# Wide zero-weight fillers in the open PV group, conv lags by modelled time, later VectorE PV

## Chip, cores, metric

One core of one Trainium2 chip. The metric is the device time of one execution in microseconds (us); lower is better. TensorE is called PE here, VectorE DVE, ScalarE ACT, as in the profile.

## The reference, cut to what matters

```python
# A: attention, S=2048, D=512, 32 heads of 16
scores = einsum("bhqd,bhkd->bhqk", q, k) * Dh**-0.5
o = softmax(scores) @ v ; a = o @ wo
# B: H3 block: short shift conv, then a causal conv of length 2048 per channel (by FFT)
kv = k_shift * v
y  = irfft(rfft(kv) * rfft(ssm_k))[:S] + kv * ssm_D
b  = q * y
return concatenate([a, b], -1)
```

2048 blocks of 128x512 scores need an exponential each. The long conv is done on PE, as 8192 small matmuls in the gaps of the attention ("lags": 4 matmuls each, one per column tile).

## The kernel before

The whole program is laid out in advance in steps T. In each step PE does scores (QK) of one chunk of 2 or 3 blocks, PV (the exponentials times `v`) of an older chunk, then background work: lags of the conv, and in some steps, called slots, a query or output projection. The sums of PV stay open in their bank over many steps, one group of sums per column tile (a strip of 32 columns) of PE's array; ACT does the exponentials (tile PT in the profile), and DVE takes one block of some chunks by a polynomial (tile PTD). Fillers are matmuls with zero weights, which compute nothing and only keep PE busy. The host code keeps a modelled time for each engine (`pe.t`, `at(handle)`) and places work by it. The score banks are two sets of three, so scores of T+1 wait for the exponentials of T-1.

```python
LAGS, PACE, END = 7, 1.08, 24
N_SLOT, MARGIN, WINDOW, BUSY = 35, 0.25, 3.4, 0.56

# pv_step: PV of DVE blocks only when modelled as ready for 0.3 us
d = [b for b in d if b in h_blk and (close or at(h_blk[b]) <= pe.t - 0.3)]

# emit_bg: conv lags of one step
st["lags"] = min(st["lags"] + PACE * st["left"] / max(NT - END - T, 1), 3.0 * LAGS)
left = min(LAGS, int(st["lags"]), int((room(T) - 0.06) / 0.055))

def warm_up(T):                       # fillers, to keep PE busy
    if T <= max(early) or T >= NT - 14:
        return
    gap = at(h_exp[T - 1]) + 0.25 - max(pe.t, at(bank_free[BGB]) + 0.12)
    lately = sum(r for t, r in pe.runs[-40:] if t > pe.t - WINDOW)
    n = min(int(gap / 0.055), 4, int((BUSY * WINDOW - lately) / 0.054))
    ...                               # n matmuls, 128 columns, into the conv bank

for T in range(NT + 3):               # (cut)
    emit_qk(T); pv_step(T); emit_bg(T); warm_up(T)
```

The softmax here doesn't subtract the row's maximum and nothing guards it: scores larger than these inputs give would overflow.

## Time and profile before

| | before |
|---|---|
| time, three runs | 924.28 to 926.37 us, median 926.11 |
| granted PE clock, mean | 0.951 |
| first to last exponential | 902.6 us, of which 77.0 us above the undisturbed period |
| stretches at half clock | 18, about 90 us |
| fillers | 234 of 128 columns, 12.5 us of streaming |

ACT bounds the kernel (94% busy, 56% of the chain that ended last); the question is why its exponentials come later than they could. The clock rows of the traces of this kernel hold only 0.5 and 1.0, and every stretch between the first and the last (34 of them) lasts a whole multiple of 3.413 us. "Half-clock time" is therefore 2 x (1 - mean granted clock) x time. "Streaming" is columns over 2.4 per ns: 512-column matmuls of the projections (L761) follow each other by 0.216 us at full clock (median in the trace of the kernel before), which is 2.37 per ns. "Standstill" is a gap of over 1.2 us on PE's matmul row after 105 us and before the tail.

### The profile page before, as it was taken

The page shows a single profiled execution, that of the slowest core. Times are in us where ns is not written, and L with a number is a line of the kernel's source. Part 1 is how long each engine was busy: PE and PEld are TensorE (multiplying, and loading weights), DVE is VectorE, ACT ScalarE, POOL GpSimd, SP SyncE. Part 2 cuts the span into 40 slices and gives each one's busy share as a digit, 9 for nine tenths or more (in the row PEclk, how much of TensorE's full clock was granted, in tenths as well). Part 3 has the DMA queues.
Part 4 walks back from the last instruction along what each step waited for, and adds up shares of the span by engine and source line. Part 5 has one row for each costly group of instructions (what it writes and reads, how often), then busy time and mean ns, then how long its engine had stood idle before and what let it go on. Part 6 is the DMA issues. An engine that isn't in the chain of part 4 may idle for free.

```text
span 921.7 us, 29467 instructions
## 1 busy us (share of the span) xinstructions
PE 752.7 (82%) x13091; PEld 331.8 (36%) x13137; DVE 781.2 (85%) x1293; ACT 867.7 (94%) x724; POOL 42.3 (5%) x62
## 2 busy tenths in 40 slices
PE   8988788888888888788887887888877888777787
PEld 3322224333334343434443333333433433333332
DVE  4788798899979698999897797889899898899972
ACT  5998999999999999999999898999999999999997
POOL 2113030000000000000000000000000000000000
PEclk9997998898999898999999799899999999999999
DMA  9743459999999999999999999899999999989610
GB/s 312 242 137 114 160 211 339 368 399 378 375 372 408 342 391 348 408 364 405 350 380 406 327 391 345 308 404 400 356 368 361 343 307 389 363 297 367 228 46 23
DMA packets 88512, 295.65 MB, mean 321 GB/s; under 512 B 11205, under 2 KB 19394, under 8 KB 88002
## 3 DMA queue, kind: packets, MB, share of 16 engines
q1 hardware_dynamic: 82114, 280.13, 81.6%
q0 software_dynamic: 3872, 12.58, 4.0%
q8 instruction: 104, 1.70, 0.7%
q10 hardware_dynamic: 2400, 1.05, 0.4%
q14 instruction: 22, 0.18, 0.1%
HBM read 287.31 MB, written 6.42 MB: 319 GB/s over the span
## 4 chain that ended last, share of the span: by engine, by line
ACT 56%; PE 24%; DVE 11%; DMA 5%; issue 3%; SPq 1%; ACTq 0%; DVEq 0%
ACT PT L562 56%; PE PS L550 8%; PE PS L639 5%; DMA WR<-kz_scratch 5%; DVE EH L599 4%; PE PS L811 3%; PE PS L761 2%; PE PS L376 2%; DVE FX L592 1%; PE PS L362 1%; PE PS L369 1%; DVE PTD L604 1%; DVE DT L708 1%; SPq L207 1%; DVE QT L391 1%
## 5 line engine op out<-in xcount | busy, mean ns | idle before, releaser
L562 ACT ACTIVATE PT<-PS 128x1536 bf16<-128x1536 f32 (+1 forms) x718 | 863.7, 1381 | 40.9 <-PE PS L550 39.7
L550 PE MATMUL PS<-QT,KTo 32*128 32x512 bf16 x2048 | 291.5, 400 | 123.6 <-ACT PT L562 108.7
L811 PE MATMUL PS<-WR,KV 128*16 128x128 bf16 (+15 forms) x8192 | 243.8, 230 | 17.9 <-DMA WR<-kz_scratch 7.0
L599 DVE SCALAR_TENSOR_TENSOR EH<-EH,FX 128x512 f32<-128x512 f32 x374 | 257.5, 705 | 0.8
L639 PE MATMUL PS<-PT,VAF 128*32 128x512 bf16 x1861 | 230.6, 409 | 10.1 <-DVE DT L708 4.8
L811 PEld LDWEIGHTS PS<-WR,KV 128*11 128x11 bf16 (+15 forms) x8192 | 173.6, 110 | 90.2 <-issue 64.7
L592 DVE TENSOR_SCALAR FX<-PS 128x512 f32<-128x512 f32 x187 | 131.6, 704 | 57.0 <-PE PS L550 56.7
L550 PEld LDWEIGHTS PS<-QT,KTo 32*128 32x128 bf16 x2048 | 71.0, 91 | 284.9 <-ACT PT L562 226.5
L604 DVE SCALAR_TENSOR_TENSOR PTD<-EH,FX 128x512 uint16<-128x512 f32 x187 | 132.0, 711 | 6.2 <-PE PS L639 5.2
L599 DVE SCALAR_TENSOR_TENSOR EH<-FX 128x512 f32<-128x512 uint16 x187 | 129.5, 702 | 0.8
L639 PEld LDWEIGHTS PS<-PT,VAF 128*32 128x32 bf16 x1861 | 54.3, 94 | 138.3 <-issue 116.0
L639 PE MATMUL PS<-PTD,VAF 128*32 128x512 bf16 x187 | 59.0, 406 | 0.0
L708 DVE STREAM_TRANSPOSE DT<-PS 128x512 f32<-128x512 f32 x31 | 22.7, 733 | 17.9 <-PE PS L639 17.5
L761 PE MATMUL PS<-WKV,OTN 128*128 128x512 bf16 x114 | 31.7, 388 | 2.7 <-issue 1.9
L828 DVE CAST YB<-PS 128x512 bf16<-128x512 f32 x32 | 22.1, 689 | 13.5 <-PE PS L811 13.3
L362 PE MATMUL PS<-xT,WQP 128*128 128x512 bf16 x107 | 28.4, 380 | 5.2 <-issue 1.9
L207 POOL DMA_DIRECT2D out_dram<-OUTA x12 | 6.6, 554 | 565.2 <-DVE OUTA L770 565.2
L970 PE MATMUL PS<-IDN,ZW 128*9 128x128 bf16 (+12 forms) x234 | 31.0, 234 | 0.6 <-PE PS L639 0.4
L391 DVE TENSOR_SCALAR QT<-PS 128x512 bf16<-128x512 f32 x32 | 22.6, 705 | 7.2 <-PE PS L362 6.6
L725 DVE STREAM_TRANSPOSE OTN<-DTN 128x512 bf16<-128x512 bf16 (+1 forms) x35 | 23.3, 674 | 0.1
L406 DVE CAST VAF<-PS 128x512 bf16<-128x512 f32 x16 | 11.1, 691 | 12.1 <-PE PS L376 12.1
L369 PE MATMUL PS<-xT,WKV 128*128 128x512 bf16 x60 | 18.1, 427 | 1.8 <-DVE QT L391 1.1
(66 smaller groups left out, 269.1 us busy)
## 6 DMA issues: line engine op xcount, KB each, us to landing
WR<-kz_scratch SPq DMA_DIRECT2D x512, 512.0 KB, 8.1
WR<-in_B_k_dram POOLq DMA_DIRECT2D x16, 256.0 KB, 4.6
kz_scratch<-WR SPq DMA_DIRECT2D x1, 2176.0 KB, 9.1
KV<-in_A_x_dram SPq DMA_DIRECT2D x4, 512.0 KB, 7.3
QN<-in_B_q_dram POOLq DMA_DIRECT2D x2, 1024.0 KB, 12.8
out_dram<-QN POOLq DMA_DIRECT2D x2, 1024.0 KB, 8.7
WR<-in_B_v_dram SPq DMA_DIRECT2D x6, 256.0 KB, 2.8
QT<-in_B_k_dram POOLq DMA_DIRECT2D x6, 256.0 KB, 4.8
```

Of the source, the lines that this page charges most:

```text
L362: return e.matmul(PS[:, bank, :], lhsT=WQP[:, dc, g, :], rhs=xT[:, dc, qb * 512:(qb + 1) * 512], start=(dc == 0), stop=(dc == 3))
L391: hh = urgent(lambda e: e.tensor_scalar(QT[:, qb % 2, g, :], PS[:, bank, :], QSCALE, None, ALU.mult), [h, h_kzt[0] if qb == 1 else None], ...
L550: ins = e.matmul(PS[:, bank, :], lhsT=KTo[32 * s:32 * s + 32, g // 2, kt * 128:(kt + 1) * 128], rhs=QT[32 * s:32 * s + 32, qb % 2, g, :], ...
L562: h_exp[T] = act.op(lambda e: e.activation(PT[:, T % R_PT, 0:n * QB], PS[:, banks[0]:banks[0] + n, :].rearrange("p b f -> p (b f)"), ACT.E ...
L592: h_f = urgent(lambda e: e.tensor_scalar(fx, PS[:, bank, :], FIX_ADD, FIX_HI, ALU.add, ALU.min), [h, h_last.get(i - R_FX)], slack=0.6)
L599: st["h"] = dve.op(lambda e: e.scalar_tensor_tensor(eh, src, (A3, A2, A1)[j], frac, ALU.add, ALU.mult), [st["h"], h_last.get(i - R_EH), h_ ...
L604: lambda e: e.scalar_tensor_tensor(out16, eh, A4, fx, ALU.mult, ALU.add),
L639: ins = e.matmul(dst, lhsT=w, rhs=rhs, start=(k == 0), stop=(k == KT - 1), tile_position=(0, 32 * s))
L708: h_t = urgent(lambda e: e.transpose(out=dt, in_=PS[:, pvb(n), :]), [h] + before, slack=0.1, us=(0.63, 0.751))
L761: ins = e.matmul(PS[:, bank, :], lhsT=OTN[:, oslot(qb * NG + g), t * 128:(t + 1) * 128], rhs=WOP[:, g, :], start=(g == 0), stop=(g == NG - 1))
L811: ins = e.matmul(PS[32 * c:32 * c + NB - n, BGB, 128 * (kk % 4):128 * (kk % 4) + 128], lhsT=KV[:, n:NB, d], rhs=WR[:, d % R_W, 128 * (NB - ...
L970: ins = e.matmul(PS[0:rows, BGB, 128 * kk:128 * kk + 128], lhsT=ZW[:, 0:rows], rhs=IDN[:, :], start=(lag == 0), stop=(lag == 0), tile_posi ...
```

## The change

The intent is to keep PE from falling to half clock, with fillers that need no bank of their own, and to spread the conv evenly.

```diff
-LAGS = 7
+LAGS = 5
-N_SLOT = 35
+N_SLOT = 36
-MARGIN = 0.25
+MARGIN = 0.4
-BUSY = 0.56
+BUSY = 0.7
+FILL_GAP = 0.25
+RATE = 3.3
+CAP = 8.0
+LATE = 0.6
-            d = [... at(h_blk[b]) <= pe.t - 0.3)]
+            d = [... at(h_blk[b]) <= pe.t - LATE)]
-        st["lags"] = min(st["lags"] + PACE * st["left"] / max(NT - END - T, 1), 3.0 * LAGS)
+        left_us = max(1.14 * (NT - END - T), 1.0)
+        st["lags"] = min(st["lags"] + min(PACE * st["left"] / left_us, RATE) * (pe.t - st["t"]), CAP)
+        st["t"] = pe.t
     def warm_up(T):
-        if T <= max(early) or T >= NT - 14:
+        if T < 3 or T >= NT - 3:
+        (n = group whose PV sum is open, s = a column tile of it; none: return)
-        gap = at(h_exp[T - 1]) + 0.25 - max(pe.t, at(bank_free[BGB]) + 0.12)
+        gap = at(h_exp[T - 1]) + 0.14 - pe.t - FILL_GAP
-        n = min(int(gap / 0.055), 4, int((BUSY * WINDOW - lately) / 0.054))
+        k = min(int(gap / 0.055), int((BUSY * WINDOW - lately) / 0.054) + 1, 4)
-        (n matmuls of 128 columns, PS[0:rows, BGB, ...], lhsT=ZW)
+        (one matmul of 128*k columns, PS[32*s:32*s+32, pvb(n), 0:128*k], lhsT=ZW,
+         start=False, stop=False; rhs = IDN repeated k times)
```

More of the change, by code (lines that the diff above doesn't have):

```diff
@@ L685, in pv_step @@
                         assert dve.n > k
-            d = [b for b in d if b in h_blk and (close or at(h_blk[b]) <= pe.t - 0.3)]
+            d = [b for b in d if b in h_blk and (close or at(h_blk[b]) <= pe.t - LATE)]
             bl = a + d
@@ L867, in bass_concat_heads__mha_block__ssm_conv_h3__prompt_kernel @@
     state = {"qd": 0, "lag": 0, "turn": False, "q": 0, "op": 0, "job": [], "started": False, "lags": 0.0,
-             "left": C // 4 * NB}
+             "left": C // 4 * NB, "t": 0.0}
     def room(T):
@@ L956, in warm_up @@
     def warm_up(T):
-        if T <= max(early) or T >= NT - 14:
+        if T < 3 or T >= NT - 3:
             return
-        gap = at(h_exp[T - 1]) + 0.25 - max(pe.t, at(bank_free[BGB]) + 0.12)
+        n = max([blk_group(b) for b in chunks[T][0]] + [0])
+        while n > 1 and not any(0 < pv_n.get((n, s), 0) < KT for s in range(4)):
+            n -= 1
+        live = [s for s in range(4) if 0 < pv_n.get((n, s), 0) < KT]
+        if not live or n in pv_done:
+            return
+        gap = at(h_exp[T - 1]) + 0.14 - pe.t - FILL_GAP
         lately = sum(r for t, r in pe.runs[-40:] if t > pe.t - WINDOW)
-        n = min(int(gap / 0.055), 4, int((BUSY * WINDOW - lately) / 0.054))
-        if n < 1:
+        k = min(int(gap / 0.055), int((BUSY * WINDOW - lately) / 0.054) + 1, 4)
+        if k < 1 or lately > BUSY * WINDOW:
             return
-        kk, lag = state["qd"] % 4, state["lag"]
-        rows = NB - lag if lag else 32
-        def fn(e):
-            ins = None
-            for _ in range(n):
-                ins = e.matmul(PS[0:rows, BGB, 128 * kk:128 * kk + 128], lhsT=ZW[:, 0:rows], rhs=IDN[:, :],
-                               start=(lag == 0), stop=(lag == 0), tile_position=(0, 0))
-            return ins
-        pe.op(fn, [h_zw, bank_free[BGB]], us=(0.06 + 0.054 * n, 0.46), run=0.054 * n)
+        s = live[0]
+        rhs = bass.AP(tensor=IDN.tensor if hasattr(IDN, "tensor") else IDN, offset=IDN[0:1, 0:1].offset,
+                      ap=[IDN[:, :].ap[0], [0, k], [1, 128]])
+        pe.op(lambda e: e.matmul(PS[32 * s:32 * s + 32, pvb(n), 0:128 * k], lhsT=ZW[:, :], rhs=rhs,
+                                 start=False, stop=False, tile_position=(0, 32 * s)),
+              [h_zw, h_idn], us=(0.06 + 0.054 * k, 0.3 + 0.054 * k), run=0.054 * k)
     def keep_busy(e):
```

## The prediction

> **What bounds the kernel now.** I read the page from its first part downwards, then the ScalarE group by form, the waits, and last the table of stretches at the places where the TensorE clock is halved.
>
> ```profile
> PE 752.7 (82%) x13091; PEld 331.8 (36%) x13137; DVE 781.2 (85%) x1293; ACT 867.7 (94%) x724; POOL 42.3 (5%) x62
> PEclk9997998898999898999999799899999999999999
> ACT 56%; PE 24%; DVE 11%; DMA 5%; issue 3%; SPq 1%; ACTq 0%; DVEq 0%
> L562 ACT ACTIVATE PT<-PS 128x1536 bf16<-128x1536 f32 x425 | 618.3, 1559 | 25.3 <-PE PS L550 24.7
> L562 ACT ACTIVATE PT<-PS 128x1024 bf16<-128x1024 f32 x293 | 312.8, 1123 | 15.5 <-PE PS L550 15.0
> ```
>
> ScalarE, which takes the exponentials (L562), is the bound: 94% busy, and 56% of the chain that ended last. The only thing it waits for is the score matmuls of L550, 39.7 us (24.7 + 15.0). Its busy time hides more, because these activations overlap: a duration of 1559 ns is not a period. So I took the 717 distances between starts of consecutive activations in the trace. The undisturbed period is 1.324 us for three blocks and 0.898 us for two; 495 of the 717 distances lie within 0.05 us of it. At these periods the 902.6 us from first to last start would be 825.6 us. The excess, 77.0 us, is all that a change can win while ScalarE keeps its work; the rest of the 921.7 us is 11 us of start and some 8 us of end.
>
> Where does the excess sit? TensorE has two clocks in this trace: 18 stretches at exactly 0.5, together about 90 us ((1 - 0.951) x 2 x 921.7), and 1.0 elsewhere. The table of stretches around three of them:
>
> ```profile
> core 0: us, PE busy (x) PEld busy (x) DVE busy (x) ACT busy (x) POOL busy (x), PEclk, DMA share, GB/s
> 295.22:298.63 3.41, 1.96 (x32) 0.71 (x29) 3.41 (x7) 3.41 (x4) 0.00 (x0) 1.00 1.05 414
> 298.63:302.05 3.42, 3.42 (x59) 1.91 (x62) 1.72 (x3) 3.42 (x3) 0.00 (x0) 0.55 1.01 398
> ...
> 571.70:575.11 3.41, 0.70 (x21) 0.36 (x23) 0.42 (x1) 0.89 (x1) 0.00 (x0) 1.00 1.02 408
> 575.11:578.53 3.42, 2.84 (x38) 1.02 (x35) 3.32 (x6) 2.71 (x3) 0.00 (x0) 0.55 1.02 418
> ```
>
> Each slow row follows a row with little PE work. The two cases differ: at 295 PE only waited for ScalarE, at 571 it stood still for 3.29 us. I counted the share of each 3.413 us window in which PE streams columns (columns over 2.4 per ns, simultaneous tiles once). Before the 17 slow stretches from 76 us to 886 us it was 0.15 to 0.50, twelve of them at or above 0.38; before a warm window its median is about 0.6, and hardly ever below 0.41. The threshold is near 0.45.
>
> The 92 activations that fall in slow stretches carry 26.4 us of excess, the other 625 carry 50.6 us (0.081 us each). At the warm rate the 92 would have 7.4 us, so the slow clock, with what caused it, costs about 19 us. Of the warm excess I could assign, by what PE did between the release of the score banks and the late scores: 14.5 us to the query and output projections in the slots (33 steps), 5.7 us to early projections, 4.6 us to conv matmuls, 3.8 us to PV, 4.5 us to standstills of PE.
>
> The waits bear this out:
>
> ```profile
> PE PS L550 <- ACT PT L562: 108.7, 258, 1.8
> ACT PT L562 <- PE PS L550: 39.7, 72, 2.6
> PE PS L811 <- DMA WR<-kz_scratch: 7.0, 9, 2.8
> PE PS L811 <- issue: 5.6, 4, 3.3
> PEld PS L639 <- DVE PTD L604: 4.0, 9, 2.2
> PE PS L639 <- DVE PTD L604: 1.9, 1, 1.9
> ```
>
> PE has room for more work (it waited 108.7 us for ScalarE before scores), but there are standstills of up to 3.3 us for a DMA or for nothing that the profile shows.
>
> [...] The trace agrees: only 0.5 and 1.0, and stretches of 3.4, 6.8 and 13.7 us. [...] the 0.45 above is mine. [...] here four L761 matmuls of 512 columns take 1.04 us and one 0.39 us, so (1.04 - 0.39)/3 = 0.217 us. [...]
>
> **The change, part by part.**
>
> 1. Fillers. Removed: 234 matmuls of 128 columns in L970, about 234 x 0.054 = 12.6 us of streaming, tied to the conv bank and allowed only between the projections and the last 14 steps. Added: one matmul of up to 4 x 128 columns per step, from step 3 to the third from the end, whenever the kernel's own clock sees a gap before ScalarE's release and the last 3.4 us hold less than 70% streaming (56% before). PE's own streaming is about 55% of a mean step of 902.6/717 = 1.26 us. If 400 to 650 steps get a filler of 0.15 to 0.2 us, that is 60 to 130 us of PE time, all meant to lie in front of a wait for ScalarE. The share then rises to 0.62 to 0.68. Windows that fell to 0.38 to 0.50 by plain waiting (nine or ten of the 17) should stay warm. Windows with a standstill (about seven, among them 136, 271, 317, 504, 571 and 720 us) should mostly still fall: with 1.6 us lost, (3.41 - 1.6)/3.41 x 0.68 = 0.36. I expect 11 of the 19 us back, and 2 us more in the steps after a slow stretch, which are still late. Sum: -13 us.
>
> 2. Conv. Lags are given by modelled time, at most 3.3 per us, saved up to 8 (21 before), at most 5 a step (7 before), and stop 0.15 us earlier. Short steps (0.90 us) get fewer lags than long ones (1.32 us). This works on the 4.6 us of warm conv lateness, on part of what follows a slot, and on the bursts of DMA requests. I take -4 us.
>
> 3. PV of VectorE blocks is sent only 0.6 us after their modelled end. The two lines PTD L604 above show 5.9 us of waiting, little of it on ScalarE's path: -1 us. The buffers come free later, which can cost some of the 187 VectorE blocks; each lost one gives ScalarE back about 0.43 us (1.324 - 0.898). I count +1 us with the added slot: its two shorter activations cost only 2 x (0.449 - 0.441) x 2 us, nothing.
>
> 4. Price of the fillers. Where PE is really later than its model, 0.2 us is put ahead of scores. There is slack of 0.5 to 0.9 us (period less the 0.39 us of scores), so it bites only after slots. I take it as inside the rounding of the other terms.
>
> Sum: 926.1 - 13 - 4 - 1 + 1 = 909 us, 1.8% faster.
>
> **Rivals.**
>
> A. The clock is the whole matter: all 19 us return, VectorE and conv are smoother still, 890 to 900 us. For it: even stretches with a standstill begin after modest shares (0.36 at 209 us). Against: fillers cannot be issued while PE itself stands still.
>
> B. The bound moves to the conv DMA. In the page 512 loads of 512 KB, and slices of up to 408 GB/s with 9 or 10 tenths of the DMA busy: 268.4 MB need 660 us at that rate, and the conv runs from 127 to 884 us, 757 us. There is 13% of room on the mean, but pacing at 3.3 lags per us asks for 3.3/16 x 2.1 MB = 432 GB/s. If the modelled arrivals get ahead of the real ones, the 7.0 us of DMA waits grow to 15 or 20 us, each wait makes a slow window, and the gain is eaten: 918 to 926 us. Against it: the model holds lags back until their modelled arrival.
>
> C. Fillers come at wrong moments: they delay scores in many steps by 0.1 to 0.2 us. A hundred such steps cost 10 to 20 us: 920 to 935 us. Against it: 495 of 717 activations start on time, so the model of time is good.
>
> D. The lateness of the slots (14.5 us) is touched by nothing here, and the standstills stay: only 5 us from the clock: 918 to 922 us. The chance of this is real.
>
> **Range and chances.** The centre is 909. A brings it to about 896, B and D to about 921; outside these I leave a tenth on either side. Two per cent faster means below 907.6, a little under the centre, so slightly less than even: 0.40. Slower by over 2% needs C or B in full: 0.03. The rest, 0.57, is within 2%.
>
> **What would show it right or wrong.** Right: granted clock 0.97 to 0.99, at most 8 slow stretches, none after a mere wait for ScalarE; a new filler group with 400 to 650 matmuls and PE busy 87 to 95%; ScalarE's wait for L550 down from 39.7 to 24 to 32 us; about 187 VectorE blocks and unchanged periods of 1.324 and 0.898 us. Standstills of over 1 us still present. Wrong: a clock still below 0.96 (zero weights or narrow fillers would not count as activity); a clock of 1.0 with the same time (lateness was never of the clock); L811's wait for DMA above 12 us (B); scores late right after a filler in many steps (C); 10 VectorE blocks more or fewer, which would move ScalarE by 4 us on its own.

That zeros added to an open PV group leave its sum alone was an assumption when the forecast was made; the changed kernel, with 234 such fillers, gives correct results. The limit near 0.45 is an estimate from the shares counted in the trace.

## The result, and the profile after

900.92 us median (898.90 to 905.34, 4 runs) against 926.24 us (4 runs). The ratio is 0.9735, 95% interval 0.969 to 0.978. Ratios here are the mean time of one kernel's fast runs over that of the other's of the same rounds, so not quite the ratio of the quoted medians. The results are correct.

From the page of the changed kernel: engines, clock, chain, then the exponentials by form, and the filler group (before, it read `x234 | 31.0, 234`):

```profile
PE 744.1 (83%) x13084; PEld 325.2 (36%) x13127; DVE 779.5 (87%) x1288; ACT 865.1 (96%) x725; POOL 42.3 (5%) x62
PEclk9997999999999999899999999999999999999999
ACT 51%; PE 19%; DVE 16%; DMA 11%; issue 2%; SPq 1%; ACTq 0%
L566 ACT ACTIVATE PT<-PS 128x1536 bf16<-128x1536 f32 x424 | 616.7, 1559 | 11.2 <-PE PS L554 10.3
L566 ACT ACTIVATE PT<-PS 128x1024 bf16<-128x1024 f32 x295 | 314.3, 1121 | 11.8 <-PE PS L554 11.4
L979 PE MATMUL PS<-IDN,ZW 128*32 128x256 bf16 (+3 forms) x234 | 69.4, 296 | 0.5 <-DVE QN L852 0.5
```

The exponentials last as long as before (1559 and 1121 ns); what shrank is ACT's idle time before them, 39.7 to 21.7 us. The count of blocks on ACT is the same but for one (186 on DVE, 187 before). From the starts of the exponentials: 882.1 us from first to last, 55.6 us of excess. Near half clock the excess went from 26.4 to 11.4 us, elsewhere from 50.6 to 44.2 us. "Near" takes in about 1.5 us on either side of each half-clock stretch, as the prediction's 92 activations do; strictly inside start 54 and 13 of them, with 22.3 and 8.9 us. The slow stretches went from 18 to 5. The two profiled runs lie 20.6 us apart (923.46 and 902.89 us), the medians 25.

The waits of the changed kernel:

```profile
PE PS L554 <- ACT PT L566: 96.2, 285, 1.0
ACT PT L566 <- PE PS L554: 21.8, 44, 1.9
PE PS L815 <- DMA WR<-kz_scratch: 15.1, 20, 1.7
```

DMA waits of the conv doubled (7.0 to 15.1 us), but the longest fell from 2.8 to 1.7 us, and PE's matmul waits on `issue` at this line went from 5.6 us (longest 3.3) to one of 0.3.

How a stretch looks, PE alone, before and after (cut out of longer views). First before, in the window that led to the slow clock at 299 us:

```profile
295.51 0.34 PE L811 MATMUL PS<-WR,KV 128*3 128x128 bf16 x12
295.88 0.39 PE L550 MATMUL PS<-QT,KTo 32*128 32x512 bf16 x3
296.20 0.39 PE L639 MATMUL PS<-PT,VAF 128*32 128x512 bf16 x2
296.20 0.39 PE L639 MATMUL PS<-PTD,VAF 128*32 128x512 bf16 x1
297.22 0.39 PE L550 MATMUL PS<-QT,KTo 32*128 32x512 bf16 x3 [0.62 <-ACT PT L562]
297.54 0.23 PE L970 MATMUL PS<-IDN,ZW 128*32 128x128 bf16 x1
298.56 0.39 PE L550 MATMUL PS<-QT,KTo 32*128 32x512 bf16 x3 [0.79 <-ACT PT L562]
```

Then the changed kernel at the same time:

```profile
295.85 0.45 PE L815 MATMUL PS<-WR,KV 128*6 128x128 bf16 x20
296.14 0.27 PE L979 MATMUL PS<-IDN,ZW 128*32 128x256 bf16 x1
296.63 0.39 PE L554 MATMUL PS<-QT,KTo 32*128 32x512 bf16 x3 [0.23 <-ACT PT L566]
296.96 0.40 PE L643 MATMUL PS<-PT,VAF 128*32 128x512 bf16 x4
297.18 0.49 PE L815 MATMUL PS<-WR,KV 128*1 128x128 bf16 x16
297.46 0.27 PE L979 MATMUL PS<-IDN,ZW 128*32 128x256 bf16 x1
```

Before, PE sat idle 0.6 to 0.8 us in front of the scores in two steps running, with one short filler; after, both steps shown have conv and a filler of 256 columns.

Over the whole run, take the clock's windows of 3.413 us (the grid of its stretches) between 76 and 870 us that ran at full clock, and the share of each in which PE streamed columns (2.4 per ns as above; overlapping matmuls count once, as the scores of one operation start 3 ns apart and take 0.39 us each). Its mean rose from 0.57 to 0.59; the lowest tenth ended at 0.45 before and 0.50 after, and windows below 0.45 fell from 22 of 207 to 6 of 225. A count that includes the half-clock windows gives nearly the same mean before and after (0.596 and 0.597), because there a matmul is counted for twice as long (in the trace of the kernel before, L761 matmuls follow each other by 0.43 us at half clock, in the two pairs that lie there, for 0.22 at full clock; a score matmul takes 0.60 us for 0.39): such a mean hides the change. The 26 windows in a recorded expectation below come from an earlier count.

### The profile page after: what moved, and what is told of

It is laid out like the page before. It is cut to its first block, busy times and chain, and to the rows that moved or that the text cites. A ratio compares the mean times of both kernels' runs of the same rounds, so it can differ in the third digit from the quotient of the medians.

```text
span 901.1 us, 29431 instructions
## 1 busy us (share of the span) xinstructions
PE 744.1 (83%) x13084; PEld 325.2 (36%) x13127; DVE 779.5 (87%) x1288; ACT 865.1 (96%) x725; POOL 42.3 (5%) x62
## 3 DMA queue, kind: packets, MB, share of 16 engines
q10 hardware_dynamic: 2400, 1.05, 0.5%
## 4 chain that ended last, share of the span: by engine, by line
ACT 51%; PE 19%; DVE 16%; DMA 11%; issue 2%; SPq 1%; ACTq 0%
ACT PT L566 51%; DMA WR<-kz_scratch 11%; DVE EH L603 6%; PE PS L554 6%; PE PS L643 4%; DVE FX L596 2%; PE PS L765 2%; PE PS L366 2%; DVE PTD L608 2%; PE PS L380 2%; SPq L211 1%; PE PS L815 1%; PE PS L373 1%; DVE DT L712 1%; DVE WR L445 1%
## 5 line engine op out<-in xcount | busy, mean ns | idle before, releaser
L554 PE MATMUL PS<-QT,KTo 32*128 32x512 bf16 x2048 | 283.3, 388 | 113.3 <-ACT PT L566 96.2
L815 PE MATMUL PS<-WR,KV 128*5 128x128 bf16 (+15 forms) x8192 | 243.9, 223 | 21.6 <-DMA WR<-kz_scratch 15.1
L643 PE MATMUL PS<-PT,VAF 128*32 128x512 bf16 x1862 | 220.9, 394 | 4.3 <-DVE DT L712 3.4
L815 PEld LDWEIGHTS PS<-WR,KV 128*7 128x7 bf16 (+15 forms) x8192 | 173.7, 108 | 92.9 <-issue 64.4
L596 DVE TENSOR_SCALAR FX<-PS 128x512 f32<-128x512 f32 x186 | 131.0, 705 | 50.6 <-PE PS L554 50.3
L979 PE MATMUL PS<-IDN,ZW 128*32 128x256 bf16 (+3 forms) x234 | 69.4, 296 | 0.5 <-DVE QN L852 0.5
L643 PE MATMUL PS<-PTD,VAF 128*32 128x512 bf16 x186 | 55.0, 386 | 0.0
L395 DVE TENSOR_SCALAR QT<-PS 128x512 bf16<-128x512 f32 x32 | 22.3, 697 | 10.4 <-PE PS L366 10.0
L979 PEld LDWEIGHTS PS<-IDN,ZW 128*32 128x32 bf16 x234 | 22.7, 97 | 2.2 <-issue 2.2
```

The source lines that it names most:

```text
L554: ins = e.matmul(PS[:, bank, :], lhsT=KTo[32 * s:32 * s + 32, g // 2, kt * 128:(kt + 1) * 128], rhs=QT[32 * s:32 * s + 32, qb % 2, g, :], ...
L596: h_f = urgent(lambda e: e.tensor_scalar(fx, PS[:, bank, :], FIX_ADD, FIX_HI, ALU.add, ALU.min), [h, h_last.get(i - R_FX)], slack=0.6)
L643: ins = e.matmul(dst, lhsT=w, rhs=rhs, start=(k == 0), stop=(k == KT - 1), tile_position=(0, 32 * s))
L815: ins = e.matmul(PS[32 * c:32 * c + NB - n, BGB, 128 * (kk % 4):128 * (kk % 4) + 128], lhsT=KV[:, n:NB, d], rhs=WR[:, d % R_W, 128 * (NB - ...
L979: pe.op(lambda e: e.matmul(PS[32 * s:32 * s + 32, pvb(n), 0:128 * k], lhsT=ZW[:, :], rhs=rhs, start=False, stop=False, tile_position=(0, 3 ...
```

## The experiments

Twelve kernels ran, all correct, beside the kernel before. "b_" starts from the kernel before, "a_" from the changed one. Several others could not be laid out at all: the changed kernel with PV at 0.3 or 0.4 us, with margin 0.25, with 7 lags a step or with the old fillers, and the kernel before with the new pacing but 35 slots, end in an error of the program's own scheduler. So the effect of taking only the later PV out of the change stays untried, and 36 slots belong to the pacing.

Theory F: the fillers do most of it. Rival P: the even pacing does. Four kernels, one part each, or the change without its fillers.

**b_newfill**: the new `warm_up` in the kernel before.
```diff
-BUSY = 0.56
+BUSY = 0.7
+FILL_GAP = 0.25
-    (old warm_up)
+    (new warm_up)
```

> The kernel before with only the new fillers (512 columns wide, into the open PV group, in all steps, 70% limit); conv pacing and VectorE PV as before. Theory F (the fillers do most of it by keeping the clock up): ratio to before 0.980 to 0.986, granted clock 0.97 or more, at most 9 slow stretches. Rival P (the even pacing of the conv does most of it; fillers are small change): ratio 0.992 to 1.000, clock 0.955 to 0.965, and the standstills of PE of over 1.2 us still there.

Ratio 0.9842 (0.9805 to 0.9879), clock 0.974 to 0.983. As F expects, but for 10 slow stretches in its trace (F allowed 9); and 6 standstills stayed.

**b_pace36**: the new pacing in the kernel before.
```diff
-LAGS = 7; MARGIN = 0.25; N_SLOT = 35
+LAGS = 5; MARGIN = 0.4; N_SLOT = 36; RATE = 3.3; CAP = 8.0
-    (lags per step)
+    (lags by modelled time)
```

> The kernel before with only the new conv pacing (by modelled time, 3.3 lags per us, 8 saved up, 5 a step, margin 0.4, 36 slots, without which it does not finish); the old narrow fillers. Theory F: ratio 0.992 to 0.998, clock 0.955 to 0.97, slow stretches still above 12. Rival P: ratio 0.978 to 0.985, clock above 0.975, few slow stretches, share of windows below 0.45 streaming down from 26 to under 10.

Ratio 0.9803 (0.9768 to 0.9837), clock 0.971 to 0.985; standstills 2, full-clock windows below 0.45 down to 13 of 220 (22 of 207 before). The ratio is as P expects, too, the windows less so (P had expected under 10). The clock rose although the program laid out fewer old fillers (135, 7.2 us of streaming, for 234). So each part alone gives more than half of the gain.

**a_nofill**: `warm_up` returns at once.
```diff
     def warm_up(T):
+        return
```

> The changed kernel without any filler. Theory F: the slow stretches come back: clock 0.94 or less, ratio to before 0.99 to 1.01. Rival P: clock about 0.96, ratio 0.980 to 0.985, most of the gain stays.

Ratio 0.9864 (0.9828 to 0.9901), clock 0.956 to 0.974. Between the two: without fillers the clock falls, but half of the gain stays.

**b_late06**: only the later PV.
```diff
-            d = [... at(h_blk[b]) <= pe.t - 0.3)]
+            d = [... at(h_blk[b]) <= pe.t - 0.6)]
```

> The kernel before with only the later VectorE PV (0.6 instead of 0.3 us after the modelled end). Both theories: ratio 0.997 to 1.003; waits of L639 for PTD down from 5.9 us to under 2. A ratio below 0.995 would make it a third cause of its own.

Ratio 0.9834 (0.979 to 0.9878): a miss for both. Its six runs spread from 901.86 to 918.28 us (the profiled one was the longest and counts as slow, so its trace explains nothing here; in it 4.1 us of the waits of L639 for PTD were left, not under 2). Three parts of 1.6 to 2.0% each add up to 5.2%, and the whole is 2.65%. Either each removes the same loss (S), or the schedule of the kernel before is an unlucky one that any reshuffling mends (U). Placebos decide: because the layout follows a model, every constant shifts it a little.

**b_slot36**: one slot more, nothing else.
```diff
-N_SLOT = 35
+N_SLOT = 36
```

> A placebo: the kernel before with 36 slots in place of 35, nothing else. Its step order shifts slightly because the modelled schedule reacts to every constant. Theory S (each of the three parts removes for itself the same loss, slow clock and late scores, so the gains do not add up): ratio to before 0.997 to 1.003. Rival U (the schedule of the kernel before is an unlucky one, and any reshuffling gains): ratio 0.983 to 0.990.

Ratio 0.9991 (0.9941 to 1.004).

**b_late033**: PV a hair later.
```diff
-            d = [... at(h_blk[b]) <= pe.t - 0.3)]
+            d = [... at(h_blk[b]) <= pe.t - 0.33)]
```

> A second placebo: the kernel before with VectorE PV at 0.33 instead of 0.30 us after the modelled end, a tenth of the step to 0.6. Theory S: ratio 0.996 to 1.003. Rival U: 0.983 to 0.990, as with 0.6 (0.983).

Ratio 0.9969 (0.991 to 1.0027). Both say S: these two reshuffled layouts gained nothing.

**a_oldpace**: the changed kernel with the old pacing.
```diff
-LAGS = 5; MARGIN = 0.4
+LAGS = 7; MARGIN = 0.25
-    (lags by modelled time)
+    (lags per step)
```

> The changed kernel with the old conv pacing (per step, up to 21 saved, 7 a step, margin 0.25), new fillers and later PV kept. Theory S: ratio to before 0.978 to 0.984, slightly better than the fillers alone (0.984) and 0.5 to 1% short of the whole change (0.9735). Rival U: no better than the fillers alone, 0.984 to 0.990, or anywhere.

Ratio 0.9768 (0.9726 to 0.981), clock 0.985 to 0.992: better than both theories expected. With fillers and later PV in place, the pacing adds nothing that can be told from the placebo that follows.

**a_late05**: a placebo of the changed kernel.
```diff
-LATE = 0.6
+LATE = 0.5
```

> A placebo of the changed kernel: VectorE PV at 0.5 instead of 0.6. Both: ratio to before within 0.970 to 0.977 if the changed kernel's time is robust. Under U it could as well be 0.980, which would show how far a reshuffling alone moves a kernel.

Ratio 0.9774 (0.9731 to 0.9817), just outside the band for robustness. Two kernels that differ by under half a per cent here should not be ranked.

**a_k1**: fillers in nearly the same places, 128 columns each.
```diff
-        k = min(int(gap / 0.055), int((BUSY * WINDOW - lately) / 0.054) + 1, 4)
+        k = min(int(gap / 0.055), int((BUSY * WINDOW - lately) / 0.054) + 1, 1)
```

> The changed kernel with each filler cut to 128 columns: 233 fillers in nearly the same places, 12.4 us of streaming instead of 30.1. Theory W (what counts for the clock is streaming time, so the width of the fillers matters): time at half clock 40 to 60 us (68 without fillers, 25 with the wide ones), ratio to before 0.979 to 0.985. Rival N (an instruction now and then is enough, the width is beside the point): 20 to 30 us at half clock, ratio 0.973 to 0.977.

Ratio 0.9793 (0.9738 to 0.9848). Mean half-clock time 35 us: less than W expected, more than N. The ratio lies in W's band, but its interval reaches into N's and holds the ratio of the whole change too: inconclusive between the two on time. On the clock the width seems to help (25 us with the wide ones, over four runs), but the single runs overlap (20 to 57 us here, 18 to 31 with the wide ones).

**a_busy09**: a higher limit for the fillers.
```diff
-BUSY = 0.7
+BUSY = 0.9
```

> The changed kernel with the streaming limit raised from 0.7 to 0.9: 267 fillers, 37.7 us of streaming. Theory W with the line through the runs so far (894.6 us + 0.31 us per us at half clock): 12 to 22 us at half clock, ratio 0.969 to 0.975. Rival L (more fillers make scores late): clock up, but ratio 0.977 or more.

Ratio 0.9758 (0.9713 to 0.9802); five of six runs at 899.84 to 900.98 us. Half-clock time 21 us, as W expects; the ratio lies just above W's band and below L's. No further gain shows, so the limit at 0.7 is enough.

**b_nofill**: the kernel before without its fillers.
```diff
     def warm_up(T):
+        return
```

> The kernel before without its own narrow fillers. Theory W: time at half clock up from 89 to 110 to 140 us, ratio 1.007 to 1.02. If the old fillers did nothing (rival: bound to the conv bank, they came at the wrong moments): ratio 0.997 to 1.003, half-clock time as before.

Ratio 0.9932 (0.989 to 0.9975): a miss for both theories. The clock did fall (mean 0.944, 103 us at half clock), and yet the kernel is faster by 0.7%, with 4 standstills for 7 and, in its trace, 33.0 us of ACT's waits for scores for 39.7. The old fillers cost more than they gave; the effect is not large beside what the placebos move (0.1 to 0.4%), but the interval excludes 1. Why they cost, the runs don't show: in the trace of the kernel before, scores right after an old filler are not later than others (mean excess 0.03 us, 0.085 us for the rest).

**a_op_busy09**: old pacing and the higher limit together.
```diff
 (a_oldpace, and)
-BUSY = 0.7
+BUSY = 0.9
```

> New fillers and later PV with the old conv pacing (0.977) and the limit at 0.9: 223 fillers, 39.9 us of streaming. If the pacing is indeed worth little once the fillers are there: 8 to 20 us at half clock, ratio 0.968 to 0.976, level with the changed kernel. If the even pacing is needed for its freedom from standstills: ratio 0.978 or more.

Ratio 0.9745 (0.9704 to 0.9787): level with the changed kernel. No version beat the changed one clearly.

What ties the runs together, means over the fast executions of a kernel, standstills from its one trace (a slow run for b_late06):

| kernel | ratio | half-clock us | standstills, us in all |
|---|---|---|---|
| before | 1 | 85 to 92 | 7, 14.2 |
| b_slot36 | 0.9991 | 94 | 8, 15.4 |
| b_late033 | 0.9969 | 76 | 7, 14.0 |
| b_nofill | 0.9932 | 103 | 4, 7.2 |
| a_nofill | 0.9864 | 68 | 3, 4.1 |
| b_newfill | 0.9842 | 38 | 6, 10.9 |
| b_late06 | 0.9834 | 63 | 4, 6.3 |
| b_pace36 | 0.9803 | 43 | 2, 2.8 |
| a_k1 | 0.9793 | 35 | 1, 1.4 |
| a_late05 | 0.9774 | 22 | 1, 1.5 |
| a_oldpace | 0.9768 | 23 | 4, 7.4 |
| a_busy09 | 0.9758 | 21 | 2, 3.5 |
| a_op_busy09 | 0.9745 | 21 | 3, 5.5 |
| after | 0.9735 | 25 | 2, 3.1 |

Over the 105 fast executions of these 14 kernels, time = 895.5 us + 0.29 x half-clock time, with a correlation of 0.93 and 3.6 us of scatter. It holds within one kernel too, where only the chance of the run differs: b_slot36 took 929.69 us at a clock of 0.937 and 918.62 us at 0.955, a slope of 0.30 over its six runs. Within the kernels, taken together, the slope is 0.25. So half-clock time is the common currency: the change saved about 64 us of it, which at 0.25 to 0.29 is 16 to 19 us of the 25. The line still is a correlation over kernels that differ in more than the clock, and it fails by up to 8 us: b_nofill lies 8 us below it, a_nofill and b_late06 4 us; b_newfill and b_late033 lie 4 us above, the kernel before 2 us. That the kernels without fillers lie low would fit a price of the fillers of some us; nothing here separates that.

What goes before a drop of the clock shows in the same 14 traces. Of the full-clock windows between 60 and 890 us, 115 streamed less than 0.41 of their time, and 113 of these were followed by half clock; of 152 at 0.41 to 0.46, 38 were; of 2894 above 0.46, two. One long gap is not needed: in the window before the slow stretch at 77 us (share 0.38) no gap exceeded 0.51 us.

The second column counts what the first leaves out. A standstill is lost time on PE at once (14.2 us in the seven of the kernel before), and all seven were followed by a slow stretch. From the trace of b_slot36, scores that belong to one operation, with no wait between them, after two bursts of conv:

```profile
569.00 0.72 PE L811 MATMUL PS<-WR,KV 128*1 128x128 bf16 x27
569.78 0.39 PE L550 MATMUL PS<-QT,KTo 32*128 32x512 bf16 x3
570.11 0.60 PE L811 MATMUL PS<-WR,KV 128*11 128x128 bf16 x28
570.70 0.39 PE L550 MATMUL PS<-QT,KTo 32*128 32x512 bf16 x2
573.81 0.38 PE L550 MATMUL PS<-QT,KTo 32*128 32x512 bf16 x1 [2.71 <-issue]
```

The three scores share one wait ahead of the first, so the third was not held by a semaphore. In the 14 traces, of 46 standstills between 140 and 880 us, 27 end 1.05 to 1.47 us after a 16 KB packet of the instruction queue has landed. Such packets land about every 7.7 us, so chance would give 2 to 3 in a band of this width (it was chosen after looking). The packets are PE's instructions, to judge by their number:

```profile
q8 instruction: 104, 1.70, 0.7%
```

The trace of the kernel before has 26,705 PE records (matmuls, weight loads and a few hundred others), 257 for each of these 104 packets. If that is so, one can count how far PE has run ahead: the PE records started when a packet lands, less 256 for each packet that landed earlier (a round figure next to the measured 257). In the kernel before this count has a median of 313 and never exceeds 431. At five of its standstills (271, 317, 356, 571 and 720 us) it was 410 to 430. In all, 21 of the 27 packets are among the three with the highest count of some 26 that landed within 100 us. In these cases PE came to a halt when it was among the furthest ahead of its packets, and went on 1.05 to 1.47 us after the next one had landed. All 21 lie in the eight traces with the old pacing, with its bursts of up to 7 lags, and none in the six with the new one. So the standstills with the highest counts are gone with the new pacing. That PE had run out of instructions in them is my reading of the count and is not shown: no run changed the fetch alone. If the packets came late, what made them so is open: the 27 themselves took 0.9 to 1.2 us, like the others (median 1.0). Many of the other standstills end with a conv load.

## Why the prediction was right, and where its steps were not

**The bound and the size of the prize.** Right. ACT stayed the bound, its periods stayed, and the whole gain is less excess (77.0 to 55.6 us). The sum of 17 us was too small by 8 us; the time, 900.9 us, lies within the range of 896 to 921, near its low end. What came, over 2% faster, had been given a chance of 0.40, less than the 0.57 for within 2%. That the range held is in part luck: the steps below were off in both directions, and one gain had no term.

**The clock term, 13 us.** The clock rose as expected: granted clock 0.986 (0.97 to 0.99 expected), 5 slow stretches (at most 8). Measured in the trace, the excess near slow stretches fell by 15.0 us; by the slopes of the runs the clock brought 16 to 19 us. The term was somewhat undersized: I charged a slow microsecond at 19/90 = 0.21 us, and the runs show 0.25 within a kernel and 0.29 across kernels.

**How the fillers do it.** This step failed. I expected 400 to 650 fillers, 60 to 130 us of streaming and PE 87 to 95% busy, with the share in a window up to 0.62 to 0.68. There were 234 fillers with 30 us of streaming, PE was busy 83%, and the mean share at full clock went only to 0.59. I assumed that gaps would be filled wherever PE waited for ACT; the code fills only what its model leaves after conv. That was enough because half clock followed the lowest windows (113 of the 115 under 0.41, 2 of 2894 above 0.46, in the count above): below 0.45 there were 6 for 22. The prediction's shares before slow stretches (0.15 to 0.50) come out lower in the recount, 0.11 to 0.43, with the same limit a little above 0.4. "None after a mere wait for ACT" did not quite hold: of the five slow stretches, that at 575 us follows a window with a share of 0.41 and no gap over 0.74 us.

**Conv pacing, 4 us, and later PV, 1 us.** Both mis-sized, and a sum was the wrong form. Alone, pacing (with 36 slots) is worth 2.0% and later PV 1.7%; with the other two parts in place pacing is worth nothing that can be told. From b_newfill to a_oldpace (later PV and 36 slots added) the ratio goes from 0.9842 to 0.9768. Each part lifts the clock (alone to 38, 43 and 63 us of half-clock time, from 85 to 92), and what one has won another cannot win again. I took later PV by its 5.9 us of PTD waits; the fast runs of b_late06 lost 26 us of half-clock time, which at 0.29 is 8 us, and the remaining 7 us of their mean gain of 15 I cannot assign.

**What stays: standstills.** I said that they would still be there and still make slow windows. They went from 7 to 2 (14.2 to 3.1 us). The prediction had no term for this; by the count above, five of the seven came when PE was 410 to 430 records ahead of its packets (median 313), in bursts that the new pacing spreads. It also counted the old fillers as harmless, and b_nofill measures them at a cost of 0.7%.

**Rivals.** A (890 to 900 us) was nearest. B's sign appeared, DMA waits of 15.1 us, above the 12 I had named, without its effect: twenty short waits instead of nine with one of 2.8 us. C (fillers that make scores late) did not happen in a size that shows: in the changed kernel's trace, away from slow stretches, 20 of 212 scores right after a filler came over 0.1 us late, against 89 of 381 others, and more fillers still (a_busy09) did not cost time beyond the noise. D's 918 to 922 us were far off, though the slots stayed about as late as before (13 to 16 us of warm excess by how one assigns it, 14.5 in the prediction).

**Blocks on VectorE.** 186 against 187, as expected, so that route moved nothing.

## What to carry to other kernels

Where PE feeds another engine and idles a little in each step, look at the distribution of its activity over the clock's windows (3.413 us here), and not only at its mean: here half clock followed 113 of 115 full-clock windows with under 0.41 of streaming, and fillers of 3% of the time, with an even conv and later PV, removed 13 of 18 slow stretches. Parts that all cure the same loss do not add up, so measure each with the others in place, and run a placebo (a constant changed by a hair) before explaining half a per cent. Measure what a filler brings: the old ones, tied to the conv bank, brought no gain all told, though that the bank was the reason is not shown. And spread bursts of small matmuls: in the eight traces with up to 28 in a step, 21 standstills ended 1.05 to 1.47 us after an instruction packet, with PE among the furthest ahead of its packets, and in the six with at most 20 none did.
